# Two transformer layers on one core: where G is summed, how M is assembled, and when q of six tiles is made

## The chip, the core and the metric

The kernel runs on one core of a Trainium2 chip. The metric is the device time of one execution in microseconds (us). Before the change it is 1361.66 us, the median of 3 runs (1360.94 to 1362.24). The engines go by the names of the profile: PE is the matrix engine, PEld its weight loads, DVE the vector engine, ACT the scalar engine, POOL the general engine and SP the queue that issues the DMAs here.

## What is computed

A block of linear attention and a dense block with a squared ReLU, each on the layer-normalized input and added to it, twice over with the same weights. The input is 2048 x 640, float32.

```python
def _A_ref(x, wqkv, wo):
    H = 32; Dh = D // H                       # 32 heads of 20
    q, k, v = qkv[0], qkv[1], qkv[2]          # x @ wqkv
    phi = lambda t: jnp.where(t > 0, t + 1, jnp.exp(t)) + 1e-6
    pq, pk = phi(q), phi(k)
    kv = jnp.einsum("bhsd,bhse->bhde", pk, v)
    z = jnp.einsum("bhsd->bhd", pk)
    num = jnp.einsum("bhqd,bhde->bhqe", pq, kv)
    den = jnp.einsum("bhqd,bhd->bhq", pq, z)[..., None] + 1e-6
    return (num / den) @ wo                   # heads side by side again
...
x = x + _A_ref(_layernorm(x, axis=-1), A_wqkv, A_wo)
x = x + _B_ref(_layernorm(x, axis=-1), B_w1, B_b1, B_w2, B_b2)   # the two lines, twice
```

The kernel never makes v. With xh the normalized x and kh = phi(k), it sums G = xh^T kh over all tokens, gets each head's kv from G and wv, and folds kv with wo into one 640 x 640 matrix M, so that the attention's output is (q / den) M.

## The kernel before

**Tiles and precision.** The 2048 tokens are 16 tiles of 128 rows. A float32 operand is split into a high part, rounded to the PE's fast format (by ACT), and a low part, the rest (by DVE: `split`, L112). A product is then three matrix instructions (`mm3`, L362: high x low, low x high, high x high). The few products that stay in plain float32 (head blocks at L864, M at L906, the sums at L821) each show up as two PE instructions in the trace.

**First stage** (L690 to L779), for each tile t. PE makes k and q of the tile together as 1280 columns in three banks of PSUM: 512, 512 and 256 wide (`kq_bank`, L523); the first two banks are one double bank of two (`ps_kq`), the third is one of two (`ps_q`), so two tiles' worth of k and q fit at once. For the tiles in LATE (9, 13 and 15) only k is made, in two halves of 320 columns (`proj`, L381). ACT takes the exponential out of PSUM, DVE makes phi = max(x,0) + min(exp,1) + eps (`phi_exp`, `phi_rest`, L468 to L482). k's phi is split into kh (`k_post`, L670), POOL adds it to `acc` for the sum over tokens; q's phi goes to DRAM (`q_store`) and comes back later as `pqt`. Beside that, the tile t+2 is normalized and turned: DVE turns 32 x 32 blocks (L343), ACT moves the blocks, 16 short instructions a tile (`blocks_move`, L346), and `xT_split` splits the result for the PE. In layer 0, ACT and DVE also convert the MLP's weights, two or three 128 x 640 pieces in a tile (`prep.high`, `prep.low`), which are kept in DRAM.

G is made in pairs of tiles (`g_unit`, L504): five units of 128 rows by 512 columns, and two units of 128 x 320 for the last 128 columns of kh, made turned, into GT. A unit is six PE instructions into one of two banks (`ps_g`), and then DVE adds the bank to G in SBUF (L521).

**Between the stages** (L806 to L963). In PE's order: half of the first late q; the sum over tokens (L821, with a matrix of ones, needs `acc`); the last pair's G; GT turned; the other half of the late q; the head blocks kv of six groups of six heads, 120 rows each and 40 in the last (L864), masked to the heads' diagonal by DVE into `kvbd`; M; the output product of four tiles (`b_out`, L643) with the sum and the normalization that follow; the two other late q, with two turns between them; then the MLP's first product. M is made by row tiles of 128 (L900 to L913): a row tile straddles two groups, so each half of it is two products that add up in PSUM, and it is split straight into the tile `uM`. Beside it, the tiles 0 to 3 of q are divided by their sums (`b_den`, `b_div`), turned and moved, as are the new x of the tiles 0 and 1.

**MLP** (L1474 on). Four groups of four tiles, 14 steps each; the remaining twelve tiles' attention output is made between its products. The change leaves this part as it is, but for the last late q's sum at L1502.

Every engine and SP's queue work in the order in which the program text issues; buffers are shared (twelve of `ftile`, eight of `xtile`, six of `utile`), and an instruction waits until its buffer is free.

Of the kernel before, what the change touches and what calls it, by code (L numbers as in the profile page):

```python
# [8 lines left out]
F32 = mybir.dt.float32  # L9
# [26 lines left out]
LATE = (9, 13, 15)  # L36
# [33 lines left out]
def kernel(  # L70
# [19 lines left out]
    ctx.enter_context(tc.manual_schedule())  # L90

# [327 lines left out]
    for layer in range(N_LAYERS):  # L419
# [12 lines left out]
        pa, pka = ExitStack(), ExitStack()  # L432
        pk = pka.enter_context(
            tc.tile_pool(name=f"ak_{layer}", bufs=1, space=bass.MemoryType.PSUM, reuse_waits="tile")
        )

        def pk_tile(tag, name, n=512):
            if tag in early_banks:
                return early_banks.pop(tag)
            return pk.tile([P, n], F32, tag=tag, name=name, bufs=1)  # L440

        def ps_kq(t):
            return pk_tile(f"kq{t % 2}", "pskq", 1024)

        def ps_q(t):
            return pk_tile(f"q{t % 2}", "psq")

        def ps_g(i):
            return pk_tile(f"g{i % 2}", "psG")


        early_banks = {}
        if layer > 0:
            early_banks = {
                tag: pk_tile(tag, "ps" + tag, n)
                for tag, n in (
                    ("g0", 512), ("g1", 512), ("q0", 512), ("q1", 512), ("kq1", 1024), ("kq0", 1024)
                )
            }
# [6 lines left out]


        def phi_exp(parts):  # L468
            e = ftile("e")
            for f, v in parts:  # L470
                nc.scalar.activation(f(e), v, AF.Exp)
            return e, parts

        def phi_rest(e, parts):

            r = ap.tile([P, D], F32, tag="r", name="r", bufs=2)
            nc.vector.tensor_scalar(e, e, 1.0, PHI_EPS, op0=ALU.min, op1=ALU.add)
            for f, v in parts:
                nc.vector.scalar_tensor_tensor(  # L479
                    out=f(r), in0=v, scalar=0.0, in1=f(e), op0=ALU.max, op1=ALU.add  # L480
                )
            return r  # L482

        def phi_psum(ps):

            e, r = ftile("e"), ftile("rl")
            nc.scalar.activation(halves_sb(e), halves(ps), AF.Exp)
            nc.scalar.activation(halves_sb(r), halves(ps), AF.Relu)
            return e, r

        def phi_sum(e, r):

            nc.vector.tensor_scalar(e, e, 1.0, PHI_EPS, op0=ALU.min, op1=ALU.add)
            nc.vector.tensor_tensor(out=r, in0=e, in1=r, op=ALU.add)
# [9 lines left out]
        def g_unit(p, i, ps):  # L504


            if i < DC:
                n, g = DM, G[:, i]
                ls, rs = slice(i * P, (i + 1) * P), slice(0, DM)
                left, right = xh, kh  # L510
            else:
                n = HD
                ls, rs = slice(DM, D), slice((i - DC) * HD, (i - DC + 1) * HD)
                left, right, g = kh, xh, GT_[:, rs]
            for t in (2 * p, 2 * p + 1):
                a, b = left[t][:, :, ls], right[t][:, :, rs]
                mm3(ps[:, :n], a[:, 0], a[:, 1], b[:, 0], b[:, 1], t % 2 == 0, t % 2 == 1)
            if p == 0:
                nc.vector.tensor_copy(g, ps[:, :n])
            else:  # L520
                nc.vector.tensor_tensor(out=g, in0=ps[:, :n], in1=g, op=ALU.add)  # L521

        def kq_bank(t, ps, b):  # L523

            s = slice(b * 512, min(b * 512 + 512, 2 * D))
            a = xT[t]
            for c in range(DC):
                mm3(
                    ps, a[:, 0, c, :], a[:, 1, c, :],
                    kq[c][:, 0, s], kq[c][:, 1, s], c == 0, c == DC - 1,  # L530
                )

        held, q_er = {}, {}

        def q_post(t):
            if t in held:
                m = 1024 - D
                psa, psb = held.pop(t)
                q_er[t] = phi_exp([
                    (lambda a: a[:, :m], psa[:, D:]),  # L540
                    (lambda a: a[:, m:], psb[:, : D - m]),
                ])

        def q_sum(t):
            if t in q_er:
                rq[t] = phi_rest(*q_er.pop(t))

        def q_store(t):
            if t in rq:
                nc.sync.dma_start(pqd[t], rq.pop(t))  # L550

        if layer == 0:

            psw = ps_kq(0)
# [12 lines left out]
            a_trans(0, ps_kq(1))  # L567
# [48 lines left out]
        def b_den(t):  # L616

            pr = ftile("pr")
            nc.vector.tensor_tensor(out=pr, in0=pq[t], in1=zbc, op=ALU.mult)
            dens[t] = den = small.tile([P, H], F32, tag="den", name="den")  # L620
            nc.vector.tensor_reduce(
                den, pr.rearrange("p (h d) -> p h d", d=DH), axis=mybir.AxisListType.X, op=ALU.add
            )

        def b_div(t):
# [6 lines left out]
            )  # L632

        def b_blocks(t):

            b_div(t)
            yzp[t] = blocks_T(pq.pop(t))
# [51 lines left out]

        for t in range(NT):  # L690
            first = t == 0 and layer == 0
            early = t == 0 and layer > 0
            q_store(t - 2)
# [11 lines left out]
            units = []  # L705
            if t >= 2:
                units = [0, 1, 2, 3] if t % 2 == 0 else [4, 5, 6]

            def unit():
                if units:  # L710
                    i = units.pop(0)
                    g_unit(t // 2 - 1, i, ps_g(i))

            q_post(t - 1)
            ps = ps_kq(t)
            if first:
                proj(ps, xT[t], wk("k"))
                r = phi_rest(*phi_exp([(halves_sb, halves(ps))]))
                pq0 = [ps_q(0), ps_g(0)]
                wq = wk("q")  # L720
                for c in range(DC):
                    for j in range(2):
                        s = slice(j * HD, (j + 1) * HD)
                        mm3(
                            pq0[j][:, :HD], xT[t][:, 0, c, :], xT[t][:, 1, c, :],
                            wq[c][:, 0, s], wq[c][:, 1, s], c == 0, c == DC - 1,
                        )
                    if c == 2:
                        a_trans(1, ps_kq(1))
                        a_stats(2)  # L730
                        a_apply(2)
                xh[t] = split_new(xt[t], "xh")
                k_post(t, r)
                rq[t] = phi_rest(*phi_exp(
                    [(lambda a, j=j: a[:, j * HD : (j + 1) * HD], pq0[j][:, :HD]) for j in range(2)]
                ))
                continue
            late = t in LATE
            if late:
                proj(ps, xT[t], wk("k"), range(3))  # L740
            else:
                kq_bank(t, ps[:, :512], 0)
# [798 lines left out]
```

## Time and profile before

| what | number |
|---|---|
| median of 3 runs | 1361.66 us |
| the profiled execution's own time | 1361.59 us |
| its span, first to last instruction | 1359.9 us |
| granted PE clock | 1.000 |
| busy: PE / PEld / DVE / ACT / POOL | 1351.8 / 1159.1 / 928.2 / 762.0 / 121.2 us |
| first stage, layer 0 and layer 1 | about 20 to 200 us, 685 to 871 us |
| between the stages | 199.8 to 261.6 us, 870.8 to 932.6 us |

How to read it: a row of the time order has the start in us, the length in us, the engine, the line of the kernel and the operation, what is written and read, the shape, and how many instructions were merged. A matrix instruction's own row lasts longer than its share of the PE, since they overlap; the share is the distance from start to start. In grouped rows stand busy us, the mean ns of one, and the idle time ahead. A row of the waits has total, number and longest. In the rows of DMA issues stand the KB of each and the median us from issue to landing.

### The profile page before, as it was taken

What the parts mean: (1) busy time and instruction counts of PE and PEld (TensorE: products, weight loads), DVE (VectorE), ACT (ScalarE), POOL (GpSimd) and SP (SyncE); (2) the same over time, 40 slices, a digit from 0 to 9 for tenths busy, and PEclk for the clock granted to TensorE, in tenths of its full rate; (3) what the DMA queues carried; (4) which work ended last, traced back from release to release, by engine and by line L of the source; (5) the groups of instructions that cost most, each with busy time, mean ns of one, the idle gap of its engine ahead of it and who ended that gap; (6) DMA issues with size and microseconds to landing.
All of it is one profiled execution on the core that took longest, in us unless ns stands there. A gap on an engine that the chain in (4) does not pass through costs nothing.

```text
span 1359.9 us, 18744 instructions
## 1 busy us (share of the span) xinstructions
PE 1351.8 (99%) x6759; PEld 1159.1 (85%) x6759; DVE 928.2 (68%) x1595; ACT 762.0 (56%) x1885; POOL 121.2 (9%) x178
## 2 busy tenths in 40 slices
PE   9999999999999999999999999999999999999998
PEld 8888888988888888888888888889888888888887
DVE  7888868687776677643367777677778667775323
ACT  4887757666646457421447677395756446464110
POOL 2122220000000000000012221200000000000000
PEclk9999999999999999999999999999999999999999
DMA  6578662483664485388521113345546646644734
GB/s 208 191 271 298 232 208 110 154 316 117 226 241 162 155 294 175 113 317 311 184 97 50 48 49 111 84 165 213 185 156 225 214 154 222 250 157 142 292 122 159
DMA packets 84359, 250.76 MB, mean 184 GB/s; under 512 B 10794, under 2 KB 19370, under 8 KB 83626
## 3 DMA queue, kind: packets, MB, share of 16 engines
q1 hardware_dynamic: 84122, 249.37, 52.9%
q8 instruction: 53, 0.87, 0.3%
q14 instruction: 40, 0.33, 0.1%
q10 hardware_dynamic: 144, 0.20, 0.0%
HBM read 193.50 MB, written 56.03 MB: 184 GB/s over the span
## 4 chain that ended last, share of the span: by engine, by line
PE 86%; ACT 5%; DVE 4%; issue 2%; POOL 1%; DMA 1%; SPq 0%; DVEq 0%; POOLq 0%
PE psh L1006 27%; PE psa L1056 22%; PE pskq L366 10%; PE pspo L366 7%; PE psG L366 6%; PE psas L1056 6%; ACT z L352 3%; PE psq L366 3%; PE pso L366 3%; PE psM L906 2%; DVE r L479 1%; PE pspo L1006 1%; DVE xT L115 1%; DMA st<-in_A_wqkv_dram 1%; DVE xh L115 0%
## 5 line engine op out<-in xcount | busy, mean ns | idle before, releaser
L352 ACT ACTIVATE z<-y 32x160 f32<-32x160 f32 x1424 | 475.9, 334 | 85.9 <-DVE y L343 69.5
L1006 PE MATMUL psh<-xTb,u 128*128 128x512 f32 x1360 | 324.5, 390 | 0.0
L1006 PEld LDWEIGHTS psh<-xTb,u 128*128 128x128 f32 x1360 | 254.2, 188 | 51.9
L1056 PE MATMUL psa<-u,h 128*128 128x512 f32 x1120 | 276.9, 390 | 0.0
L1056 PEld LDWEIGHTS psa<-u,h 128*128 128x128 f32 x1120 | 208.5, 188 | 41.0 <-DVE h L1021 0.3
L1018 ACT ACTIVATE hr<-psh,b1sb 128x512 f32<-128x512 f32 x102 | 70.1, 687 | 292.1 <-PE psh L1006 285.3
L1019 DVE TENSOR_TENSOR hr<-hr 128x512 f32<-128x512 f32 x104 | 71.8, 690 | 222.6 <-ACT hr L1018 222.2
L366 PE MATMUL pskq<-kq,xT 128*128 128x512 f32 (+1 forms) x960 | 211.9, 372 | 0.4 <-DVE xT L115 0.2
L366 PEld LDWEIGHTS pskq<-kq,xT 128*128 128x128 f32 x960 | 171.6, 188 | 30.6 <-DVE xT L115 0.9
L366 PE MATMUL psG<-kh,xh 128*128 128x512 f32 x468 | 117.3, 392 | 0.6 <-DVE GT L521 0.3
L366 PEld LDWEIGHTS psG<-kh,xh 128*128 128x128 f32 x468 | 86.2, 188 | 18.7 <-DVE kh L680 0.9
L327 POOL TENSOR_SCALAR rs<-mv 128x1 f32<-128x1 f32 x64 | 29.4, 459 | 810.6 <-DVE mv L325 810.6
L1056 PE MATMUL psas<-h,u 128*128 128x512 f32 x280 | 79.0, 390 | 0.0
L366 PE MATMUL psq<-kq,xT 128*128 128x256 f32 (+1 forms) x540 | 75.2, 291 | 0.9 <-DVE kq L115 0.9
L366 PEld LDWEIGHTS psq<-kq,xT 128*128 128x128 f32 x540 | 72.5, 190 | 2.6 <-DVE kq L115 1.2
L1021 DVE TENSOR_TENSOR h<-hr,h 128x512 fp32r<-128x512 f32 x104 | 72.1, 693 | 3.6
L677 POOL TENSOR_TENSOR acc<-acc,r 128x640 f32<-128x640 f32 x30 | 47.2, 1574 | 268.9 <-DVE r L479 268.9
L366 PE MATMUL pspo<-uM,pT 128*128 128x320 f32 x408 | 66.2, 309 | 0.0
L366 PEld LDWEIGHTS pspo<-uM,pT 128*128 128x128 f32 x408 | 62.3, 188 | 1.9
L1056 PEld LDWEIGHTS psas<-h,u 128*128 128x128 f32 x280 | 52.2, 188 | 10.8 <-DVE h L1032 0.4
L673 ACT ACTIVATE kh<-r 128x640 fp32r<-128x640 f32 x32 | 23.8, 743 | 64.5 <-DVE r L479 64.5
L521 DVE TENSOR_TENSOR G<-psG,G 128x512 f32<-128x512 f32 x70 | 46.8, 670 | 17.2 <-PE psG L366 17.0
(150 smaller groups left out, 1610.7 us busy)
## 6 DMA issues: line engine op xcount, KB each, us to landing
u<-kept_w SPq DMA_DIRECT2D x184, 640.0 KB, 4.4
x<-x SPq DMA_DIRECT2D x48, 320.0 KB, 4.8
kept_w<-uprep SPq DMA_DIRECT2D x23, 640.0 KB, 4.7
pqt<-pq SPq DMA_DIRECT2D x32, 320.0 KB, 4.7
x<-xr SPq DMA_DIRECT2D x32, 320.0 KB, 2.4
pq<-r SPq DMA_DIRECT2D x26, 320.0 KB, 2.3
st<-in_B_w_dram SPq DMA_DIRECT2D x22, 320.0 KB, 5.0
kept_kq<-kq SPq DMA_DIRECT2D x10, 640.0 KB, 6.8
```

The lines of the kernel that those rows point to most:

```text
L327: nc.gpsimd.tensor_scalar(rs, mv[:, 1:2], LN_EPS, None, op0=ALU.add)
L352: nc.scalar.activation(zv[j * B32 : (j + 1) * B32, :, i, :], yv[i * B32 : (i + 1) * B32, :, j, :], AF.Copy)
L366: nc.tensor.matmul(ps, a, b, start=first and i == 0, stop=last and i == 2)
L521: nc.vector.tensor_tensor(out=g, in0=ps[:, :n], in1=g, op=ALU.add)
L673: nc.scalar.activation(u[:, 0], r, AF.Copy)
L677: nc.gpsimd.tensor_tensor(out=acc, in0=acc, in1=r, op=ALU.add)
L906: nc.tensor.matmul(ps[:, j * 512 : j * 512 + HD], kvbd[c][:n, o : o + P], vo["o", c][:n, j * HD : (j + 1) * HD], start=c == cs[0], stop=c ...
L1006: nc.tensor.matmul(ps, a[:, d, :], bb[:, d, :], start=d == 0 and i == 0, stop=d == DC - 1 and i == len(seq) - 1,)
L1018: nc.scalar.activation(r, ps, AF.Relu, bias=b1sb[:, c : c + 1])
L1019: nc.vector.tensor_tensor(out=r, in0=r, in1=r, op=ALU.mult)
L1021: nc.vector.tensor_tensor(out=h[:, 1], in0=r, in1=h[:, 0].bitcast(F32), op=ALU.subtract)
L1056: nc.tensor.matmul(ps, l, r, start=first and k == 0, stop=last and k == len(a) - 1)
```

## The change

Four things change together, in both layers.

**G adds up in PSUM.** PSUM becomes one tensor of eight banks with fixed use. Banks 3 to 7 hold the five 128 x 512 parts of G from the first tile to the last; each tile adds three instructions to each (`g_part`), for the tile before the current one. DVE's additions of G go; at the end ACT copies the five banks to SBUF. GT is still made in pairs and added by DVE. k and q of a tile use banks 0, 1 and 2 in turn, and GT's products go into the same three. phi is worked in parts, as each bank is full (`Phi`).

**Six late tiles** in each layer: 9, 11, 12, 13, 14, 15 in layer 0, and 8, 9, 11, 13, 14, 15 in layer 1. Their q is made in halves of 320 columns (`late_q`), two ahead of the sum over tokens and ten more between the steps that follow.

**M by groups of heads.** For each of the six groups, two products with all 640 columns of wo make its rows of M (`m_make`). Group 0's go straight to M; the others are split into a scratch tile, and DMAs copy them into the row tiles of M. The loads of the MLP's weights are issued behind these.

**Side work in finer pieces.** Division, turns and block moves of the tiles 0 to 3 are queued (`side_work`) and taken out between the steps; the weight conversion is three pieces in the tiles 2 to 5 and two in 6 to 11. The output product of the tiles 0 and 1 runs in two turns: row tiles 0 to 2 of M for both, then 3 and 4 for both.

The core of the diff (`+` and `-` as usual):

```diff
-LATE = (9, 13, 15)
+LATE = ((9, 11, 12, 13, 14, 15), (8, 9, 11, 13, 14, 15))
+PREP = {t: 2 if t > 5 else 3 for t in range(2, 12)}
...
+    PS = psum.tile([P, 8 * 512], F32, name="PS", tag="PS", bufs=1)
+    def bank(i, n=1):
+        return PS[:, 512 * i : 512 * (i + n)]
+    XB, GB = (0, 1, 2), (3, 4, 5, 6, 7)
...
+        def g_part(t, i):
+            ps = bank(GB[i])
+            a, b = xh[t][:, :, i * P : (i + 1) * P], kh[t][:, :, :DM]
+            mm3(ps, a[:, 0], a[:, 1], b[:, 0], b[:, 1], t == 0, t == NT - 1)
...
+            ps = part(t, 0, n0, bank(XB[0]))
+            gs(0 if t == 1 and layer == 0 else 2)
             move(t + 1)
+            f.exp(0, ps)
...
+                a_apply(t + 2)
+                yza[t + 2] = blocks_T(xt[t + 2])
+            f.rest()
+            gt = t % 2 == 0 and t > 0
+            if gt and is_late:
+                gt_part(t // 2 - 1, 0, bank(XB[2]))
+            ps = part(t, n0, D if is_late else 1024, bank(XB[1]))
             if t + 1 in yza:
                 xT_split(t + 1, yza.pop(t + 1)[1])
...
+                prep.high()
+            for _ in range(4):
+                prep.low()
...
+            f.exp(n0, ps[:, : D - n0])
+            if not is_late:
+                fq.exp(0, ps[:, D - n0 :])
+            f.rest()
+            if not is_late:
+                fq.rest()
             xh[t] = split_new(xt[t], "xh")
+            if gt and not is_late:
+                gt_part(t // 2 - 1, 0, bank(XB[0]))
+            gs(1)
+            if is_late:
+                gs(1)
             else:
+                ps = part(t, 1024, 2 * D, bank(XB[2]))
+                gs(1)
+            k_post(t, f.r, [lambda: a_stats(t + 3)])
+            if gt:
+                gt_part(t // 2 - 1, 1, bank(XB[2 if is_late else 1]))
+            gs(DC)
...
+        late_q(2)
...
+            nc.tensor.matmul(psz[j], ones, acc[:, j * HD : (j + 1) * HD], start=True, stop=True)
...
+        b_den(0)
+        for i in range(DC):
+            g_part(NT - 1, i)
+            nc.scalar.activation(G[:, i], bank(GB[i]), AF.Copy)
+        for j in range(2):
+            gt_part(NT // 2 - 1, j, xbank())
+        b_blocks(0)
+        late_q(1)
...
+        def m_make(c):
+            mb.append(mb.pop(0))
+            ps = bank(mb[-1], 2)
+            n, o = head_rows(c), HR * c
+            for j in range(2):
+                nc.tensor.matmul(
+                    ps[:n, j * 512 : j * 512 + HD], kvbd[c][:n, :n],
+                    vo["o", c][:n, j * HD : (j + 1) * HD], start=True, stop=True,
                 )
+            u = M[0] if c == 0 else xtile("Mc")
+            hi, lo, src_ = halves_sb(u[:n, 0]), halves_sb(u[:n, 1]), halves(ps[:n])
+            nc.scalar.activation(hi, src_, AF.Copy)
+            nc.vector.tensor_tensor(out=lo, in0=src_, in1=hi.bitcast(F32), op=ALU.subtract)
+            if c > 0:
+                m, r = divmod(o, P)
+                k = min(P - r, n)
+                nc.sync.dma_start(M[m][r : r + k].bitcast(F32), u[:k].bitcast(F32))
+                if k < n:
+                    nc.sync.dma_start(M[m + 1][: n - k].bitcast(F32), u[k:n].bitcast(F32))
...
+        late_q(1)
...
+        for c in range(NH):
+            m_make(c)
+            run_side(1)
+            b_step(3)
+            if c == 2:
+                late_q(1)
...
         wu.free = 3
         wu.load_ring()
-        for m in range(DC):
-            ps = ps2("psM")
-            cs = [c for c in range(NH) if HR * c < P * (m + 1) and HR * c + head_rows(c) > P * m]
-            for j in range(2):
-                for c in cs:
...
+        late_q(1)
...
+        for i in range(2):
+            po[i] = bank(4 + 2 * i, 2)
+            proj(po[i], pT[i], M, range(3))
+            run_side(2)
...
+        for i in range(2):
+            proj(po[i], pT.pop(i), M, range(3, DC))
```

More of the change, by code (lines that the diff above doesn't have):

```diff
@@ L688, in move @@
                 moved[t] = n
+        late = LATE[layer]
+        q_end = None
         for t in range(NT):
@@ L732 @@
                 xh[t] = split_new(xt[t], "xh")
[L733 to L736, printed above, removed]
+                k_post(t, fk.r)
+                fq.rest()
+                nc.sync.dma_start(pqd[0], fq.r)
                 continue
[L738 to L742, printed above, removed]
@@ L743, with gs @@
-            for _ in range({2: 2, 3: 2, 4: 2, 5: 3, 6: 2, 7: 2, 8: 3, 9: 2, 10: 2, 11: 2, 12: 2}.get(t, 0) if layer == 0 else 0):
-                prep.high()
+            g = list(range(DC)) if t > 0 else []
+            def gs(n):
+                for _ in range(min(n, len(g))):
+                    g_part(t - 1, g.pop(0))
+            if q_end:
+                q_end()
+                q_end = None
+            is_late = t in late
+            f, fq = Phi(rtile()), None if is_late else Phi(rtile())
@@ L843 @@
[L843 to L851 removed]
+            for _ in range(PREP.get(t, 0) if layer == 0 else 0):
+                prep.high()
+            for _ in range(4):
+                prep.low()
+            for _ in range(PREP.get(t + 1, 0) if layer == 0 else 0):
+                prep.load()
```

454 lines of the change are left out of this document (172 added, 282 removed).

## The prediction

> **What bounds the kernel now.** I read the page's busy times first, then the list of TensorE's waits, then busy times by stage, then TensorE's rows in order of time.
>
> ```profile
> span 1359.9 us, 18744 instructions
> ...
> PE 1351.8 (99%) x6759; PEld 1159.1 (85%) x6759; DVE 928.2 (68%) x1595; ACT 762.0 (56%) x1885; POOL 121.2 (9%) x178
> ```
> ```profile
> PE psz L821 <- POOL acc L677: 0.5, 1, 0.5
> PE ps L821 <- POOL acc L677: 0.5, 1, 0.5
> ```
> ```profile
> 20.28:199.80 179.52, 178.84 (x929) 154.43 (x930) 148.67 (x254) 133.39 (x317) 40.30 (x43) 1.00 0.68 233
> 199.80:222.44 22.64, 22.05 (x153) 19.85 (x151) 17.78 (x32) 11.98 (x32) 3.77 (x3) 1.00 0.07 22
> ...
> 685.41:871.00 185.59, 185.59 (x974) 161.75 (x973) 134.09 (x231) 119.76 (x294) 40.42 (x41) 1.00 0.26 80
> ```
>
> The columns of the last view are length, then busy time of PE, weight load, DVE, ACT and POOL, the granted clock, DMA share and GB/s. PE is busy 99%; the two waits that lie in the code the change touches are the 0.5 us for the sums. The first stage (20.28 to 199.80, and 685.41 to 871.00 in layer 1) leaves PE idle for 0.7 and 0.0 us; DVE is busy for 148.67 of layer 0's 179.52, ACT for 133.39. So the G additions that leave DVE buy no time by themselves: no wait of PE is theirs. A busy PE row need not be PE at its pace, so I checked pace by start to start:
>
> ```profile
> 49.33 3.56 PE L366 MATMUL pskq<-kq,xT 128*128 128x512 f32 x15
> 52.73 1.04 PE L366 MATMUL psG<-xh,kh 128*128 128x320 f32 x6
> 53.60 1.96 PE L366 MATMUL psq<-kq,xT 128*128 128x256 f32 x15
> 55.40 1.04 PE L366 MATMUL psG<-xh,kh 128*128 128x320 f32 x6
> ```
> ```profile
> 199.80 2.36 PE L366 MATMUL psq<-kq,xT 128*128 128x320 f32 x15
> 202.63 1.34 PE L821 MATMUL psz<-acc,ones 128*128 128x320 f32 x4 [0.47 <-POOL acc L677]
> 203.57 2.15 PE L366 MATMUL psG<-xh,kh 128*128 128x320 f32 x12
> ...
> 206.95 0.71 PE L337 MATMUL psT<-ident,GT 128*128 128x128 f32 x5
> 207.42 5.75 PE L366 MATMUL psG<-kh,xh 128*128 128x512 f32 x24
> 213.00 2.36 PE L366 MATMUL psq<-kq,xT 128*128 128x320 f32 x15
> 215.20 5.71 PE L864 MATMUL pskv<-G,uraw 128*120 128x120 f32 x50
> ...
> 222.44 11.62 PE L906 MATMUL psM<-uraw,kvbd 120*128 120x320 f32 x40
> 233.99 17.86 PE L366 MATMUL pso<-uM,pT 128*128 128x320 f32 x120
> ```
>
> Fifteen 512-wide products take 3.40 us (52.73 - 49.33), that is 0.227 each; fifteen 256-wide 1.80 (0.120); fifteen 320-wide 2.20 (215.20 - 213.00; 0.147). The M rows stand out: 40 instructions for 20 products, in 11.55 us, 0.289 each. Layer 1's 185.59 us hold 13 x 8.60 + 3 x 4.40 for k and q, and 7 pairs of 30 x 0.227 + 12 x 0.147 for G: 111.8 + 13.2 + 60.0 = 185.0. PE is at its pace all through, so the change is worth what it takes from PE's stream, less the waits it makes.
>
> **The change part by part**, against the profiled execution's own 1361.6 us (span 1359.9, and 1.7 around it; the median of the runs shown is 1361.7, the same).
>
> *M by groups.* Before, each of 5 row tiles of M takes two groups of heads for two halves: 20 products, 40 instructions. After, each of 6 groups makes its own rows: 12 products, 24 instructions, as wide as before. 24 x 0.289 = 6.93, so 4.62 a layer goes: **-9.24**.
>
> *Six late tiles instead of three.* An ordinary tile costs 3.40 + 3.40 + 1.80 = 8.60 of PE. A late one makes k and q in 320-wide halves: 4 x 2.20 = 8.80. Three more in each of two layers: 6 x 0.20 = **+1.2**.
>
> *G in five banks.* The count stays: 16 tiles x 5 x 3 products 512 wide, and 96 320-wide for GT. DVE loses its 35 G additions a layer,
>
> ```profile
> L521 DVE TENSOR_TENSOR G<-psG,G 128x512 f32<-128x512 f32 x23 | 15.2, 660 | 0.0
> ```
>
> 0.66 us each; by the windows above PE waited on none, so 0. Five copies on ACT come at the end; GT (1.76) and a late half (2.20) on PE cover them, and if that cover were gone the last copy would hold PE for 0.7. What it takes away is the second set of banks for k and q: three banks now rotate. I laid one ordinary tile out from its start: part one to 3.40, two G products to 4.76, part two to 8.16, GT 0.88, G 0.68, part three 1.80, G 0.68, GT 0.88, G 0.68; GT is in even tiles alone, so 12.0 us in odd tiles, 13.8 in even ones. Bank one is wanted again 4.8 us after it is written at the earliest (by GT), bank two after 4.0, bank three a tile later. ACT has eight block moves (2 x 1.37, row below), the exponential, the turned x and up to three weight conversions to do ahead of part two's exponentials, each about 0.7 like the 640-wide M rows below; it comes through at 7.6, before part two ends. By the same laying out DVE frees bank two at about 10.3; it is wanted at 12.2. The closest deadline is the low part of k: the next tile's G wants it 3.4 us into that tile, 15.4 in an odd tile, and I get 13.7. So I take 0, with 1.7 us of slack; the other end is rival B. GT's products and the exponentials wait behind nobody else on their engines if that holds.
>
> *The wait for the sums.* Two late halves (4.40) now run ahead of the sum over tokens, so its 0.47 us, once a layer, goes: **-0.9**. Next would be the low part of the last k, which G wants 5.3 us after the stage and which, laid out in the same way, is there after 1.6.
>
> *M's pieces move by DMA.* This is the new wait. Groups straddle row tiles, so five of the six are split into a scratch tile and copied to M by nine transfers on SP's queue. Each waits on SP for its low part, and behind them wait six weight loads, the next x tiles and pq of tile 4: the weights are issued at about 36 and wanted at 66, so they bear it. I count from the stage's end. PE: 4.40 + 0.94 + 3.40 + 1.76 + 2.20 + 0.47 + 7.24 + 2.20 = 22.6 at the first group; 3.47 for three groups, 2.20 late half, 3.47, 2.20: the output product begins at 34.0 and wants row tile 2 (group 3's last rows) 1.8 later, at 35.8. ACT and DVE:
>
> ```profile
> 227.84 0.68 ACT L114 ACTIVATE uM<-psM 128x640 fp32r<-128x640 f32 x1
> 228.54 1.37 ACT L352 ACTIVATE z<-y 32x160 f32<-32x160 f32 x4
> 229.94 0.70 ACT L114 ACTIVATE uM<-psM 128x640 fp32r<-128x640 f32 x1
> ```
> ```profile
> 231.17 0.81 DVE L115 TENSOR_TENSOR uM<-psM,uM 128x640 fp32r<-128x640 f32 x1
> ```
>
> ACT's step is 2.10 us (229.94 - 227.84), above PE's 1.16, so ACT sets the pace: high parts of groups 0 to 3 end at 24.6, 26.7, 28.8 and, behind a late exponential, 31.3; the low part of group 3 at 32.1. For the copy no row shows SBUF to SBUF; the nearest are
>
> ```profile
> u<-kept_w SPq DMA_DIRECT2D x184, 640.0 KB, 4.4
> ```
> ```profile
> u<-kept_w SPq DMA_DIRECT2D x6, 640.0 KB, 8.9
> ...
> pq<-rl SPq DMA_DIRECT2D x1, 320.0 KB, 2.3
> ```
>
> (the second fence is of the 11 us around M, 226 to 237, where six loads queue up). A group is 600 KB in two transfers of 5 KB rows, so I take 4.4, the whole run's row of nearly that size and row length; the ends are 2.3 and 8.9. At 4.4 it lands at 36.6: PE waits 0.8. The later groups land at 38.5 and 39.5, and are wanted at 40 and later. **+1.6** in both layers; by the ends 0 and 10.6.
>
> [...]
>
> *Way to the MLP.* ACT has, from 36.2 on, fifteen block-move groups of 1.37, six splits of about 0.65 and seven half exponentials of about 0.4: 27.3 us, to 63.5; two of the splits wait for PE's turns at 61.7 and 64.3. The MLP's first product could start at 66.5 by PE, and DVE gives the last low part at about 66.8: **+0.6** in two layers.
>
> Sum: 1361.6 - 9.24 + 1.2 - 0.9 + 1.6 + 0.6 = **1354.8 us**.
>
> **The rivals.**
>
> *A, the copies land late (slower).* If M's copies see what the six queued loads saw, 8.9 us, PE waits 5.3 at row tile 2 instead of 0.8: 9.0 more, 1363.8. A PE that stops so long may come back slow, as at the start of this trace:
>
> ```profile
> 1.42 5.64 PE L558 MATMUL pskq<-ident 128*128 128x128 f32 x30 [1.42 <-POOL ident masks.py:199]
> ...
> 7.43 1.80 PE L558 MATMUL pskq<-ident 128*128 128x128 f32 x15
> ```
>
> Thirty turns took 5.64 where, at the later 0.12 each, they take 3.6: 2.0 lost. Twice that gives 1367.8. It decides from a landing of 9.2 us, or from about 7.2 if the restart is paid. For it: the queue's own row. Against: the weight loads stand behind the copies now, so less queues up. [...]
>
> *B, three banks are too few (slower).* The loop runs from the end of part two over exponential, sum and low k to the next tile's G, then 1.36 + 3.40 of PE back to part two. I have 5.5 + 4.8 = 10.3 against a mean period of 12.9. In before:
>
> ```profile
> 182.97 3.56 PE L366 MATMUL pskq<-kq,xT 128*128 128x512 f32 x15
> 186.37 2.88 PE L366 MATMUL psG<-kh,xh 128*128 128x512 f32 x12
> ```
> ```profile
> 190.85 1.60 DVE L680 TENSOR_TENSOR kh<-r,kh 128x640 fp32r<-128x640 f32 x1 [0.21 <-ACT kh L673]
> ```
>
> the bank is full at 186.37 and low k is there at 192.45, 6.1 later. The loop binds from 8.1. At 9, by weight conversions and block moves that end up ahead of it, PE waits 0.9 in each of the 18 ordinary tiles behind the first: 16 us, 1371. Against: DVE has lost 0.66 x 2.5 a tile.
>
> *C, half of the gain goes into small waits.* Copies at 6 us (1.6 more a layer), a tail on ACT 1 us longer, G waiting 0.5 us in some late tiles, where PE's period falls to 7.8 while ACT has 8.4: together some 6, 1361. Within 0.2%.
>
> *D, nothing waits.* Copies at 3 us, an even tail: 1361.6 - 9.24 + 1.2 - 0.9 = 1352.6, and 0.7 less if the first stage's idle goes too. If M's products were not fewer in the machine (a 120-wide weight costing more), nothing would be won: 1361.6 + 1.2 = 1363; the rows of 120-wide weights at 0.11 (50 in 5.55 us) speak against it.
>
> **How the numbers follow.** Forecast (1352.8 to 1358.9) 0.62, D 0.07, C 0.14, A 0.07, B 0.10. A measurement of this kernel tells 0.2%, 2.7 us, from no change: faster means below 1358.9, slower above 1364.4. Faster 0.69, same 0.14, slower 0.17. For 8 in 10 the range takes in the forecast, D and C, up to the point where A begins: 1351.8 to 1364.3.
>
> **What would show it.** M's rows: 24 instructions a layer in about 6.9 us of PE. The DVE rows of G adds gone but for GT's. In the list of waits, PE waiting for a DMA of M, near 0.8 us a layer; the wait for the sums gone. The first stage about 9 us shorter (three tiles' q of 4.2 leaves it, 3.4 of G comes in), with PE idle under 1 us there. I am wrong if the first stage shows PE waiting on kh or on a bank in every tile, if the wait on M is over 3 us, or if M's 24 instructions take 11 us.

## The result, and the profile after

The change makes the kernel 0.2% slower: 1363.92 us, the median of 22 runs (1362.23 to 1365.58), against 1361.61 us for the kernel before (22 runs, 1360.94 to 1362.24). The ratio is 1.0017, with a 95% interval of 1.0010 to 1.0024. The forecast was 1354.8.

The profiled execution took 1362.51 us, and its span is 1360.3. The head of its page:

```profile
span 1360.3 us, 19010 instructions
...
PE 1344.3 (99%) x6817; PEld 1161.5 (85%) x6817; DVE 910.4 (67%) x1617; ACT 770.8 (57%) x1931; POOL 122.8 (9%) x174
```

PE is busy for 7.5 us less than before (1351.8), and the span is 0.4 us longer. So work did leave PE, and waits took its place. The list of PE's waits (in all, times, longest) says which:

```profile
PE PS L379 <- DMA uM<-Mc: 8.2, 4, 2.9
...
PE PS L379 <- DVE kh L653: 0.8, 1, 0.8
PE PS L987 <- DVE xTb L128: 0.6, 2, 0.3
```

The wait for the sums (0.47 a layer) is gone, and the output product now waits 8.2 us for the copies of M. The first stage has no new wait of size. Busy time by stretch, columns as in the prediction:

```profile
19.00:190.00 171.00, 170.10 (x908) 149.22 (x908) 139.29 (x255) 134.95 (x328) 44.04 (x44) 1.00 0.70 242
686.00:871.00 185.00, 185.00 (x990) 162.94 (x990) 126.38 (x236) 125.54 (x315) 44.98 (x42) 1.00 0.24 77
```

PE is idle there for 0.9 us in layer 0 and for nothing in layer 1 (whose stretch runs on 10 us past the end of its first stage, at 860.8). Between the stages, PE's rows of layer 0 in order of time (in brackets the idle time ahead of a row):

```profile
189.39 4.56 PE L379 MATMUL PS<-kq,xT 128*128 128x320 f32 x30
193.79 1.24 PE L801 MATMUL PS<-acc,ones 128*128 128x320 f32 x4
...
211.98 3.39 PE L862 MATMUL PS<-uraw,kvbd 120*120 120x320 f32 x12
214.97 2.61 PE L379 MATMUL PS<-kq,xT 128*128 128x320 f32 x15
217.42 3.52 PE L862 MATMUL PS<-uraw,kvbd 120*120 120x320 f32 x12
220.86 2.47 PE L379 MATMUL PS<-kq,xT 128*128 128x320 f32 x15
223.17 1.92 PE L379 MATMUL PS<-uM,pT 128*128 128x320 f32 x12
227.94 4.63 PE L379 MATMUL PS<-uM,pT 128*128 128x320 f32 x30 [2.85 <-DMA uM<-Mc]
234.07 2.87 PE L379 MATMUL PS<-uM,pT 128*128 128x320 f32 x18 [1.50 <-DMA uM<-Mc]
...
260.32 1.89 PE L987 MATMUL PS<-xTb,u 128*128 128x512 f32 x7 [0.29 <-DVE xTb L128]
```

M's products take 2.99 + 3.44 = 6.43 us of PE (211.98 to 214.97, 217.42 to 220.86) where they took 11.55. The output product then runs 12 instructions, waits 2.85 for row tile 2, and waits 1.50 more for the last rows. In the chain that ended last, the second wait is one piece:

```profile
225.32 8.62 DMA uM<-Mc
```

The last copy is issued at 225.32 and lands at 233.93. From 213 up to that point the chain is nearly all ACT's splits and block moves. In layer 1 a second loss joins the wait. First PE's rows, then the stretches around them with the granted clock:

```profile
897.44 4.64 PE L379 MATMUL PS<-uM,pT 128*128 128x320 f32 x30 [0.98 <-DMA uM<-Mc]
904.91 4.41 PE L379 MATMUL PS<-uM,pT 128*128 128x320 f32 x18 [2.83 <-DMA uM<-Mc]
909.15 2.36 PE L379 MATMUL PS<-kq,xT 128*128 128x320 f32 x15
```
```profile
904.00:906.00 2.00, 1.09 (x6) 1.12 (x7) 0.00 (x0) 1.73 (x6) 0.00 (x0) 0.86 0.97 379
906.00:908.00 2.00, 2.00 (x9) 2.00 (x8) 1.53 (x3) 0.00 (x0) 0.00 (x0) 0.50 1.01 410
908.00:910.00 2.00, 2.00 (x13) 2.00 (x12) 0.97 (x3) 0.00 (x0) 0.79 (x2) 0.79 1.03 408
```

The eighteen products behind the wait take 4.24 us from start to start (904.91 to 909.15) where layer 0's took 2.71 (234.07 to 236.78): the granted clock falls to 0.50, and 1.5 us go.

Why the copies land late is seen in the DMA columns (the last two: busy share of the 16 engines, GB/s) of the stretch in which they run:

```profile
220.00:223.00 3.00, 3.00 (x18) 2.33 (x17) 2.80 (x6) 2.89 (x7) 0.00 (x0) 1.00 0.78 237
223.00:226.00 3.00, 2.09 (x15) 1.82 (x13) 2.35 (x5) 2.93 (x9) 0.00 (x0) 1.00 1.00 227
226.00:229.00 3.00, 1.06 (x7) 1.09 (x8) 0.32 (x1) 2.90 (x10) 0.00 (x0) 1.00 0.80 195
229.00:232.00 3.00, 3.00 (x23) 3.00 (x22) 0.82 (x1) 2.90 (x9) 0.00 (x0) 1.00 1.00 198
...
235.00:238.00 3.00, 3.00 (x23) 3.00 (x22) 1.92 (x4) 0.00 (x0) 0.62 (x2) 1.00 1.01 405
```

From 220 to 232 the DMA engines are busy for 0.78 to 1.00 of the time and move only 195 to 237 GB/s. Behind the copies, when the weight loads run (235 to 238), a share of 1.01 moves 405. A group of M is 600 KB, so at 215 GB/s, about the middle of those rows, it takes 2.9 us, while ACT brings a group every 2.1 (the prediction's step). By this estimate the queue falls behind by 0.8 us with every group.

**Theory.** M's copies are bound by the bytes through DMA engines that move only about half of those 405 GB/s here: the wait follows from the rate, not from the latency of one copy. Rivals: the weight loads queued behind them slow them down; the source in SBUF is slow; ACT's work on the way to the MLP is the limit, and PE would wait there if it did not wait for M; something else of the change costs the time, and the copies only show it.

### The profile page after: what moved, and what is told of

The parts are those of the page before. It is cut to its first block, busy times and chain, and to the rows that moved or that the text cites. A ratio compares the mean times of both kernels' runs of the same rounds, so it can differ in the third digit from the quotient of the medians.

```text
span 1360.3 us, 19010 instructions
## 1 busy us (share of the span) xinstructions
PE 1344.3 (99%) x6817; PEld 1161.5 (85%) x6817; DVE 910.4 (67%) x1617; ACT 770.8 (57%) x1931; POOL 122.8 (9%) x174
## 4 chain that ended last, share of the span: by engine, by line
PE 93%; ACT 3%; DMA 2%; DVE 1%; issue 0%; SPq 0%; POOL 0%; DVEq 0%
PE PS L379 36%; PE PS L987 27%; PE PS L1037 27%; ACT z L365 2%; DMA uM<-Mc 1%; PE PS L849 1%; ACT Mc L868 0%; DMA st<-in_A_wqkv_dram 0%; ACT e L475 0%; PE PS L1051 0%; DVE r L483 0%; DVE kq L128 0%; ACT xTb L127 0%; DVE e L482 0%; ACT kh L646 0%
## 5 line engine op out<-in xcount | busy, mean ns | idle before, releaser
L987 PE MATMUL PS<-xTb,u 128*128 128x512 f32 x1400 | 333.8, 390 | 0.6 <-DVE xTb L128 0.6
L987 PEld LDWEIGHTS PS<-xTb,u 128*128 128x128 f32 x1400 | 261.6, 188 | 54.6 <-DVE xTb L128 1.1
L379 PE MATMUL PS<-kq,xT 128*128 128x320 f32 (+2 forms) x1635 | 296.1, 333 | 1.0 <-DVE kq L128 0.9
L379 PEld LDWEIGHTS PS<-kq,xT 128*128 128x128 f32 x1635 | 260.1, 188 | 28.7 <-DVE kq L128 1.1
L1037 PE MATMUL PS<-u,h 128*128 128x512 f32 x1120 | 276.8, 390 | 0.0
L1037 PEld LDWEIGHTS PS<-u,h 128*128 128x128 f32 x1120 | 208.5, 188 | 40.8
L1000 DVE TENSOR_TENSOR hr<-hr 128x512 f32<-128x512 f32 x104 | 71.7, 690 | 219.1 <-ACT hr L999 218.5
L379 PE MATMUL PS<-kh,xh 128*128 128x512 f32 x480 | 126.0, 393 | 0.8 <-DVE kh L653 0.8
L379 PE MATMUL PS<-uM,pT 128*128 128x320 f32 x648 | 104.9, 312 | 8.2 <-DMA uM<-Mc 8.2
L379 PEld LDWEIGHTS PS<-uM,pT 128*128 128x128 f32 x648 | 99.3, 190 | 11.0 <-issue 7.9
L379 PEld LDWEIGHTS PS<-kh,xh 128*128 128x128 f32 x480 | 86.9, 188 | 16.1 <-DVE kh L653 1.6
```

Of the source, the lines that this page charges most:

```text
L379: nc.tensor.matmul(ps, a, b, start=first and i == 0, stop=last and i == 2)
L987: nc.tensor.matmul(ps, a[:, d, :], bb[:, d, :], start=d == 0 and i == 0, stop=d == DC - 1 and i == len(seq) - 1,)
L1000: nc.vector.tensor_tensor(out=r, in0=r, in1=r, op=ALU.mult)
L1037: nc.tensor.matmul(ps, l, r, start=first and k == 0, stop=last and k == len(a) - 1)
```

## The experiments

**Weight loads held back.** The ring's first weight loads wait until tile 0's output product has been added to x.

```diff
-        wu.free = 3
-        wu.load_ring()
+        gate = dram.tile([1, 16], F32, name=f"gate_{layer}", tag=f"gate_{layer}")
...
+        nc.sync.dma_start(gate, xr[0][:1, :16])
+        wu.free = 3
+        wu.load_ring()
```

> The changed kernel, but the first three weight loads that follow M's copies on the queue are held back until the output product of tile 0 has been added (a 64-byte store of that sum stands ahead of them). Theory 1 (M's copies run at half the rate of loads, and share the DMA engines with the weight loads behind them): the second wait on M (1.5 us in layer 0, 2.8 in layer 1) and the slow clock after it go, the first wait (2.9 and 1.0) stays: 1357 to 1359.5. Theory 2 (ACT is the limit between the stages, and PE's wait for M only stands where it would otherwise wait for ACT): the first MLP product waits for its x instead, 1362.5 to 1364.

Measured: 1363.13 us (1360.55 to 1364.17, 11 runs), ratio to before 1.0009 (1.0000 to 1.0018). Waits, then the stretches:

```profile
PE PS L379 <- DMA uM<-Mc: 7.3, 4, 2.6
```
```profile
226.00:229.00 3.00, 2.12 (x14) 2.15 (x15) 0.82 (x2) 2.90 (x9) 0.00 (x0) 1.00 0.85 213
229.00:232.00 3.00, 2.52 (x18) 2.26 (x16) 0.83 (x1) 2.90 (x9) 0.00 (x0) 1.00 0.97 245
...
235.00:238.00 3.00, 3.00 (x23) 3.00 (x22) 1.92 (x4) 0.00 (x0) 0.75 (x2) 1.00 0.23 40
```

The loads are gone (40 GB/s at 235), and the DMA engines still run at 213 to 245 GB/s with a share of 0.85 to 0.97. A store of 320 KB and two loads of x stand behind the copies here too, but they are issued from 226.89 on; from 219 to 226, ahead of them, the copies move 233 GB/s at a share of 0.87, where the changed kernel has 241 at 0.92. The waits fall from 8.2 to 7.3 us; the second wait of layer 0 ends at 233.94 as it did at 234.07, with the copies issued 0.3 to 0.6 us later, and in layer 1 the eighteen products behind a stop of 2.64 us are slow still (4.10 us). The loads behind account for about a ninth of the waits, so this rival falls as the main cause.

**More PE work ahead of the output product.** Two late halves are moved forward to stand where PE waited.

```diff
@@ behind M's six groups
-        late_q(1)
+        late_q(3)
```

> The changed kernel, but three late halves instead of one between M and the output product, so two fewer behind it. Theory 1: the copies land when they did, PE has 4.4 us more to do meanwhile, the first wait goes and under 1 us of the second stays in each layer: 1356.5 to 1360, if the two halves that cover ACT's tail are not missed. Theory 2: the wait moves to the first MLP product, 1362.5 to 1364.5.

Measured: 1365.52 us (1364.64 to 1366.36, 8 runs), ratio 1.0028 (1.0018 to 1.0038). There is no wait on M any more:

```profile
PE PS L987 <- DVE xTb L128: 6.4, 2, 3.2
PE PS L379 <- DVE rl L483: 1.7, 2, 0.9
```

The wait has moved to the MLP's first product, 3.2 us a layer, plus 0.9 a layer for a bank. From the end of the output product to that product it is 22.8 us here (238.00 to 260.77) and 23.5 in the changed kernel (236.78 to 260.32): the sum, the normalization, the turns and the block moves of the new x need that long, and the late halves were PE's work in that time. So the late halves can't cover M's landing for nothing: once M is covered, the way of x is the next limit.

**Both together**: the gate of the first, and `late_q(2)` in place of `late_q(1)`.

> Both: the three weight loads held back as in the first, and two late halves between M and the output product. Theory 1: PE waits under 1 us a layer for M, the clock stays full: 1353 to 1356, near the forecast on record. Theory 2: 1362 or more, with several us of waiting for x at the first MLP product.

Measured: 1366.02 us (1364.03 to 1368.14, 6 runs), ratio 1.0031 (1.0019 to 1.0043). M is still waited for, 3.4 us in both layers together, and x is waited for 3.0 us in each: the waits for M and for x are paid side by side.

**M by row tiles as before, the rest of the change kept.** Twenty products, split straight into M, no copies; `kvbd` has zeros beside its blocks for it, as it had before.

```diff
-        def m_make(c):
+        def m_make(m):
...
+            cs = [c for c in range(NH) if HR * c < P * (m + 1) and HR * c + head_rows(c) > P * m]
...
-            u = M[0] if c == 0 else xtile("Mc")
...
-                nc.sync.dma_start(M[m][r : r + k].bitcast(F32), u[:k].bitcast(F32))
...
+            u = M[m]
+            split(halves_sb(u[:, 0]), halves_sb(u[:, 1]), halves(ps))
...
-        for c in range(NH):
+        for c in range(DC):
```

> The changed kernel with M made by row tiles as before (20 products a layer, split straight into M, no copies); all else as changed. Theory 1: 9.2 us of PE come back, the waits of 8.2 and the slow clock (1.8 in the profile, some 1.4 more in the median) go: 1361 to 1363, with no wait on M and a narrow spread of runs. Theory 2: PE's extra work is hidden behind ACT: the same as the changed kernel, 1363.5 to 1364.5, and the wait for x at the first MLP product goes.

Measured: 1361.28 us (1360.82 to 1361.58, 11 runs), ratio 0.9997 (0.9988 to 1.0006). PE's rows:

```profile
212.73 6.62 PE L868 MATMUL PS<-uraw,kvbd 120*128 120x320 f32 x24
218.94 2.61 PE L379 MATMUL PS<-kq,xT 128*128 128x320 f32 x15
221.40 5.06 PE L868 MATMUL PS<-uraw,kvbd 120*128 120x320 f32 x16
226.38 2.46 PE L379 MATMUL PS<-kq,xT 128*128 128x320 f32 x15
228.68 8.96 PE L379 MATMUL PS<-uM,pT 128*128 128x320 f32 x60
```

M costs 6.21 + 4.98 = 11.19 us here, and the output product runs its 60 instructions without a gap. G in five banks, six late tiles and the finer side work cost nothing together and gain nothing that can be told. So groups save 11.19 - 6.43 = 4.76 us a layer, 9.5 in both, and the copies take all of it back: 8.2 of waits and 1.5 of slow clock in the profiled run.

**M's transfers read from DRAM.** The nine transfers keep their rows, order and waits; they read kept weights in place of the scratch tile, so M doesn't hold the product. A store of 64 bytes from the scratch tile ahead of each group keeps the wait for the split. What the row counts leave idle can be read in the changed kernel: while the 112 rows of group 1 move (219.1 to 220.1) mostly 16 packets are under way at once, at a share of 0.94; with the 104 rows of group 2 (221.3 to 223.3) it is mostly 13, at 0.80; from 228 to 229, where by the order of issue the 88 and 40 rows move, 12 or 13, at 0.74.

```diff
-                nc.sync.dma_start(M[m][r : r + k].bitcast(F32), u[:k].bitcast(F32))
+                gate = dram.tile([1, 16], F32, name=f"gate_{layer}_{c}", tag=f"gate_{layer}_{c}")
+                nc.sync.dma_start(gate, u[:1, 1, :16].bitcast(F32))
+                w = kept["w1", 7 + c].rearrange("p (j n) -> p j n", j=2)
+                nc.sync.dma_start(M[m][r : r + k].bitcast(F32), w[:k])
...
-                    nc.sync.dma_start(M[m + 1][: n - k].bitcast(F32), u[k:n].bitcast(F32))
+                    nc.sync.dma_start(M[m + 1][: n - k].bitcast(F32), w[k:n])
```

> The changed kernel, but the nine transfers into M take their rows from a DRAM tensor of the same shape (weights of the MLP) instead of from the scratch tile in SBUF; a 64-byte store of the scratch tile ahead of each group keeps the issue times. Leaves out that M holds the product. Theory 1a (a copy from SBUF to SBUF is slow because both ends are in SBUF): about 400 GB/s as the weight loads have, landing in 4 to 5 us, waits on M under 1 us a layer. Theory 1b (it is slow by its row counts, 88, 104, 40, which leave some of the 16 DMA engines without a share): some 200 GB/s as before, waits as before, 4 us a layer.

Measured: 1367.3 us in one run, at a mean granted clock of 0.996 (before beside it: 1361.54).

```profile
PE PS L379 <- DMA uM<-kept_w: 8.9, 4, 3.0
```
```profile
226.00:229.00 3.00, 1.33 (x9) 1.25 (x9) 0.82 (x2) 2.89 (x10) 0.00 (x0) 1.00 0.91 212
229.00:232.00 3.00, 3.00 (x23) 3.00 (x22) 0.57 (x1) 2.90 (x9) 0.00 (x0) 1.00 1.02 218
```

The rate is the same 212 to 218 GB/s at a share of 0.91 to 1.02, and so is the wait. The source in SBUF is not what is slow.

**Even rows.** Groups 1 to 4 move in one transfer of 112 rows each, from row 0 to row 0. Group 5's rows are left out, M is zeroed first and doesn't hold the right rows.

```diff
-            if c > 0:
-                m, r = divmod(o, P)
...
+            if 0 < c < DC:
+                nc.sync.dma_start(M[c][:112].bitcast(F32), u[:112].bitcast(F32))
...
+        for u in M:
+            nc.gpsimd.memset(u.bitcast(F32), 0.0)
```

> The changed kernel, but groups 1 to 4 are copied from SBUF to SBUF as one transfer of 112 rows each (7 rows for each of 16 engines), group 5 not at all, M zeroed first by POOL; 2.3 MB instead of 2.7. Leaves out that M holds the right rows. Theory 1a: still about 200 to 230 GB/s, the last copy lands about 1.5 us sooner than in the changed kernel. Theory 1b: about 400 GB/s, landing in 4 to 5 us each, waits on M under 1 us a layer.

Measured: 1352.73 us in one run, with 0.6 us of waits on M and a landing of 4.1 to 6.2 us:

```profile
223.00:226.00 3.00, 3.00 (x23) 3.00 (x22) 2.38 (x4) 2.94 (x8) 0.00 (x0) 1.00 1.00 286
226.00:229.00 3.00, 3.00 (x22) 3.00 (x21) 0.53 (x2) 2.90 (x10) 0.00 (x0) 1.00 0.90 239
```

In the first stretch, with nearly only M's copies under way, they move 286 GB/s at a full share, a quarter more than the 227 of the changed kernel in the same stretch. In the second the weight loads come in. The time can't be read as that of the rate alone: each row tile of M hangs on one group here, and fewer bytes move. Three more kernels, with one run of each, take the rate apart. They leave out group 5 and zero M as well, M's content is wrong in them, and their edits are shown against the even rows.

**Large pieces only**: rows 8 to 120, 16 to 120, 24 to 120 and 32 to 120 as in the change, the small pieces left out.

```diff
-                nc.sync.dma_start(M[c][:112].bitcast(F32), u[:112].bitcast(F32))
+                k = 8 * c
+                nc.sync.dma_start(M[c][: n - k].bitcast(F32), u[k:n].bitcast(F32))
```

> Of the nine transfers only the four large ones are left (112, 104, 96 and 88 rows, out of the scratch tile from row 8, 16, 24 and 32, into M from row 0); the small ones and group 5's are left out, and M is zeroed first, so M's content is incomplete. Read from it is the DMA rate in 217 to 235 us and the landing. If row counts that leave engines idle or the shifted rows make the transfers slow, the rate stays near the 200 to 230 GB/s at full share of the changed kernel. If it is the small pieces, it is at 290 to 320 GB/s, as with four transfers of 112 rows from row 0, and the landing is near 4 us.

**Small pieces and 80 rows**:

```diff
-                nc.sync.dma_start(M[c][:112].bitcast(F32), u[:112].bitcast(F32))
+                k = 8 * c
+                nc.sync.dma_start(M[c - 1][P - k : P].bitcast(F32), u[:k].bitcast(F32))
+                nc.sync.dma_start(M[c][:80].bitcast(F32), u[:80].bitcast(F32))
```

> Groups 1 to 4 are moved in a small transfer each (8, 16, 24, 32 rows, as in the changed kernel) and one of 80 rows from row 0 to row 0; the rest of M is zeroed and group 5's is left out, so M's content is incomplete. Bytes: 400 rows of 5 KB, 2.0 MB, against 2.3 MB for four of 112 rows. If the small pieces, or the rows at the far end of a tile, make it slow, the rate at full share is 200 to 240 GB/s; if they do not, it is near 290 to 320.

**All 128 rows, from DRAM**:

```diff
-                nc.sync.dma_start(M[c][:112].bitcast(F32), u[:112].bitcast(F32))
+                gate = dram.tile([1, 16], F32, name=f"gate_{layer}_{c}", tag=f"gate_{layer}_{c}")
+                nc.sync.dma_start(gate, u[:1, 1, :16].bitcast(F32))
+                w = kept["w1", 7 + c].rearrange("p (j n) -> p j n", j=2)
+                nc.sync.dma_start(M[c].bitcast(F32), w)
```

> Groups 1 to 4 are replaced by one transfer each of all 128 rows from weights kept in DRAM, at the place in the queue where the changed kernel issues M's; group 5's is left out; M's content is wrong. If only a transfer's rows decide, the rate at full share is that of the weight loads, near 400 GB/s, and the landing is 2 to 3 us behind the issue. If it is this stretch of the kernel (something else on the same memory), it stays near 300 GB/s or lower, and the landing at 4 us or more.

The stretches of the three, in this order:

```profile
223.00:226.00 3.00, 3.00 (x22) 2.87 (x21) 2.39 (x4) 2.94 (x8) 0.00 (x0) 1.00 0.94 218
226.00:229.00 3.00, 3.00 (x22) 3.00 (x22) 0.61 (x2) 2.90 (x10) 0.00 (x0) 1.00 0.95 215
```
```profile
223.00:226.00 3.00, 2.94 (x21) 2.68 (x19) 2.53 (x4) 2.94 (x8) 0.00 (x0) 1.00 0.84 223
226.00:229.00 3.00, 2.87 (x20) 2.90 (x20) 0.82 (x2) 2.89 (x9) 0.00 (x0) 1.00 0.99 224
```
```profile
220.00:223.00 3.00, 3.00 (x17) 1.95 (x16) 2.88 (x5) 2.92 (x7) 0.00 (x0) 1.00 0.87 280
223.00:226.00 3.00, 3.00 (x23) 3.00 (x22) 2.31 (x3) 2.92 (x8) 0.00 (x0) 1.00 0.87 266
```

Their times are 1353.16, 1354.38 and 1352.88 us, with 0.8, 1.2 and 0.8 us of waits on M. A single stretch depends on which transfers it catches. Put at a full share (GB/s over share), the stretch from 223 to 226 gives 227 in the changed kernel, 232 with large pieces alone and 265 with small ones beside 80 rows; but the changed kernel's stretch just before gives 304 (237 / 0.78). So here are the first 7 us of the copies (in the table's order from 218, 218, 219, 218 and 218 in layer 0, and from 889, 886, 887, 885 and 885 in layer 1), at a full share:

| kernel | layer 0 | layer 1 |
|---|---|---|
| as changed | 219 / 0.84 = 261 | 208 / 0.80 = 260 |
| large pieces alone | 216 / 0.80 = 270 | 224 / 0.80 = 280 |
| small pieces and 80 rows | 202 / 0.85 = 238 | 203 / 0.86 = 236 |
| 112 rows | 246 / 0.78 = 315 | 229 / 0.74 = 309 |
| 128 rows, from DRAM | 238 / 0.78 = 305 | 249 / 0.79 = 315 |

The small pieces aren't needed for the slow rate, since the large ones have nearly the same alone. Transfers of 112 or 128 rows run at 305 to 315, the others at 236 to 280, in both layers. Even whole tiles stay under the 405 of the weight loads a little later. So the way a group is cut decides part of the rate, and something else at this place another part. Which property of the rows it is, the number, the shift between source and target, or both, isn't settled by these runs, nor is the rest of the gap.

**Half the bytes.** The group's product leaves PSUM in one copy on DVE, moves into M as plain float32, and is split there.

```diff
-            u = M[0] if c == 0 else xtile("Mc")
-            hi, lo, src_ = halves_sb(u[:n, 0]), halves_sb(u[:n, 1]), halves(ps[:n])
-            nc.scalar.activation(hi, src_, AF.Copy)
-            nc.vector.tensor_tensor(out=lo, in0=src_, in1=hi.bitcast(F32), op=ALU.subtract)
+            u = xtile("Mc", F32)[:, 0]
+            nc.vector.tensor_copy(halves_sb(u[:n]), halves(ps[:n]))
+            raw.append(u if c == 0 else M[c][:, 1].bitcast(F32) if c < DC else None)
...
-                nc.sync.dma_start(M[m][r : r + k].bitcast(F32), u[:k].bitcast(F32))
+                nc.sync.dma_start(raw[m][r : r + k], u[:k])
...
+        def m_split(m):
+            split(M[m][:, 0], M[m][:, 1], raw[m])
...
+            if c > 2:
+                m_split(c - 3)
...
+        m_split(3)
+        m_split(4)
```

> The changed kernel, but a group's product is taken out of PSUM by one DVE copy and moved into M as plain float32 (half the bytes, no wait for ACT), and each row tile is split in M after its pieces have landed. If M's copies set the end of the output product, and the x of the first tiles follows 23 us behind it: copies start 2 us sooner and move in half the time, PE waits under 1 us a layer for M, 1353 to 1356. If the way of x behind the product is the limit whatever M does: 1361 or more, with the wait at the first MLP product.

Measured: 1355.53 us (1354.88 to 1355.72, 5 runs), ratio 0.9955 (0.9941 to 0.9969). It beats both kernels, the one before by 6.0 us. Its waits, PE's rows, one stretch and the landing:

```profile
PE PS L993 <- DVE xTb L128: 1.6, 2, 0.9
...
PE PS L379 <- DVE uM L128: 0.6, 2, 0.3
```
```profile
223.73 2.27 PE L379 MATMUL PS<-uM,pT 128*128 128x320 f32 x12
226.32 7.30 PE L379 MATMUL PS<-uM,pT 128*128 128x320 f32 x48 [0.32 <-DVE uM L128]
```
```profile
223.00:226.00 3.00, 2.91 (x19) 2.38 (x17) 3.00 (x5) 2.92 (x8) 0.00 (x0) 1.00 0.55 143
```
```profile
DMA to landing us min/median/max: 2.1/2.4/2.8
```

No wait on a DMA of M is left, and the kernel leaves nothing out. If the way of x were the limit, 1361 or more was expected; x is waited for 0.8 us a layer. The engines are busy for 0.55 of the stretch: a group's 300 KB take 1.4 us even at 215 GB/s and fit into the 2.1 between groups, so nothing queues. The same row counts and shifts land in 2.1 to 2.8 us instead of 5.4 to 6.9 (the same view of the changed kernel):

```profile
DMA to landing us min/median/max: 5.4/6.2/6.9
```

Two things change at once, since a copy no longer waits for ACT's high part. The issues tell them apart; the last copy's row, in the changed kernel and here:

```profile
225.32 0.77 SPq L873 DMA_DIRECT2D uM<-Mc  x1
```
```profile
225.56 0.77 SPq L872 DMA_DIRECT2D uM<-Mc  x1
```

The first copy is issued at 216.69 and 216.92, so the copies start no sooner here; what falls is the time to landing. At a full share the rate isn't higher either (143 / 0.55 = 260). This carries the theory: it is the bytes against the rate.

## Why the prediction was wrong, step by step

- **M by groups, -9.24: right.** 6.43 us of PE a layer against 6.93 counted; beside the row-tile version it saves 9.5.
- **Six late tiles (+1.2), the sums (-0.9), the way to the MLP (+0.6): right in kind.** The sums' wait is gone, the MLP's first product waits 0.3 us a layer. With M as before these terms and G in banks make 1361.28, where the sum without M's two terms has 1361.6 + 1.2 - 0.9 + 0.6 = 1362.5: 1.2 too much. (The whole sum of the forecast comes to 1354.86.)
- **G in five banks at nothing: right.** PE is idle for 0.9 us in layer 0's first stage and for none in layer 1's. Rival B doesn't occur: PE waits once for kh, 0.8 us, and not in every tile.
- **The plan of PE: right.** Counted from the stage's end at 189.39, M starts at 22.59 (22.6 was laid out), and the output product at 33.78 (34.0).
- **"M's pieces move by DMA", +1.6: this step failed.** The copies were issued as laid out (group 3's at 32.25 and 33.08 from the stage's end, where its low part was to be there at 32.1), but I gave each group the 4.4 us landing of a weight load, as if copies were independent. The landings are 5.4 to 6.9 us where the trace shows them, and 8.6 for the last piece on the chain. Row tile 2 is there at 227.9, 38.5 from the stage's end instead of 36.6, and the last rows at 44.5 instead of 39.5. PE waits 8.2 us in both layers together instead of 1.6, and layer 1 loses 1.5 us at half clock behind its waits: 6.6 + 1.5 = 8.1 us, against the 7.7 between the profiled run and the forecast. That ACT's step of 2.1 us hands 600 KB to the queue each time, so that some 290 GB/s would be needed, was in the rows of before; I took a latency where a rate was needed, and the prediction's own sign of being wrong, a wait on M over 3 us, came (4.4 us in layer 0, 3.8 in layer 1).
- **Idle engines are only a part of the slow rate.** The changed kernel has a share of 0.80 at 212 GB/s with 104 rows under way (221.3 to 223.3), but also 1.00 at 227 (223 to 226): there the engines are busy and slow.
- **Rival A came near in its time (1363.8), and in part by its mechanism.** It had the copies fare like six queued loads and PE come back slow. The copies do queue, but on one another, at a lower rate than the loads; holding the loads back gives 0.9 us of 8.2. It put 5.3 us on row tile 2 alone, where PE waits 2.85 and 0.98. The bounds of the landing, 2.3 to 8.9, held.
- **The range held the time, but not by a mechanism that it was drawn for.** Rival C had copies at 6 us, near the 5.4 to 6.9 measured, and priced them at row tile 2 as well. The waits for the last rows (1.50 and 2.83) and the half clock are in neither the forecast nor C.
- **A stop under 3 us was enough for half clock.** The stop of 2.83 us in layer 1 was followed by a granted clock of 0.50; in layer 0, stops of 2.85 and 1.50 were not (18 products in 2.71 us). In the trace of the changed kernel the granted clock is 1.00 for 901.119 us from its first record at 4.306, 0.50 for 3.413 (905.425 to 908.838), 1.00 for 450.559, and 0.50 again from 1359.398 on; 901.119 and 450.559 are 264 and 132 times 3.4133. Counted in such stretches, layer 1's stop lies whole in one (902.01 to 905.42: PE busy 0.58 of 3.41), and a border at 226.17 cuts layer 0's into 1.08 and 1.77. Ahead of the second fall PE is idle for 2.89 us of such a stretch (1355.99 to 1359.40), and in no other behind the first record for more than 1.77. Two other kernels have slow products behind such a stop as well: with the weight loads held back, behind a stop of 2.64 us in layer 1 (18 in 4.10 us), and with M's transfers from DRAM, behind one of 3.04 in layer 0 (18 in 4.94, at a granted clock of 0.50 from 235 to 238). That the idle time within one such stretch decides is my estimate from these stops; no run tried it alone.

The median lies 1.4 us above the profiled run. Of the 22 runs, the six with a mean granted clock of 0.998 average 1362.6 us, the sixteen with 0.996 or 0.997 average 1364.4. By estimate, one more stretch of 3.41 us at half clock takes 0.00125 off the mean and costs 1.7 us, which fits. The row-tile kernel and the half-bytes kernel, which don't wait for copies, ran at 0.999 or 1.000 in all of their 16 runs. That the slower clock comes from the waits is thus likely for the rest too, but only the profiled run's 1.5 us is shown.

## What to carry to other kernels

Price a series of copies by bytes over rate against the interval at which they are produced, not by the latency of one; take the rate from a row with the same rows and tiles, and if there is none, from well below the best rate in the trace. If a copy can move data before it is doubled (here before the split in two halves), move it then. Ahead of moving filler work to cover a wait, look at what that filler covered in its old place: here it covered the way of x to the MLP, and the wait came back there.

## What the runs showed of the hardware

Copies of part tiles in a row kept the DMA engines 0.78 to 1.02 busy at 195 to 245 GB/s, whether they read SBUF or DRAM. At a full share, groups cut in shifted or part rows moved 236 to 280 GB/s over the first 7 us, transfers of 112 and 128 rows 305 to 315, in both layers; the weight loads reached 405 at 1.01 a little later. A row of 5 KB thus took 16 x 5.12 KB / 227 GB/s = 0.36 us of an engine in the changed kernel (223 to 226), and 0.20 behind the stage. What makes the difference stays open.

In the changed kernel the granted clock fell to 0.50 for 3.413 us behind layer 1's stop of 2.83 us and stayed at 1.00 behind layer 0's of 2.85. Cut into stretches of 3.413 us from the clock's first record, the first leaves 2.83 us of idle PE in one stretch, the second 1.08 and 1.77 in two. So by estimate from this one trace, where a border falls decides whether such a stop costs clock.
